# Rows of x for experts 1 to 7: spread over partition groups by DMA and transposed in 32x32 blocks on VectorE instead of on TensorE

## The chip, the cores and the metric

The kernel runs on one core of a Trainium2 chip. The core has five engines, each with its own instruction stream: TensorE (PE in the profile, its weight loads PEld), VectorE (DVE), ScalarE (ACT), GpSimd (POOL) and SyncE (SP), which here only issues DMAs. They meet through semaphores. The metric is the device time of one execution in microseconds; the time of a kernel is the median of its runs.

## The reference, cut to what matters

First a linear attention with decay (batch 4, 8 heads, 768 steps, head size 48) is computed; its output, 3072 rows of 384, is the x of a mixture of 8 experts. Every row goes to its two best experts:

```python
top2 = np.argpartition(-noisy_logits, 2, axis=1)[:, :2]
...
for e in range(E):
    for k in range(2):
        mask = top2[:, k] == e
        h = np.maximum(x[mask] @ w1[e], 0.0)          # 384 -> 1024
        out[mask] += top2_w[mask, k, None] * (h @ w2[e])   # 1024 -> 384
```

Everything is float32. The change is in the expert part.

## The kernel before, in words

**Attention part, up to about 190 us.** 24 blocks of 128 rows go through the attention; each block's x is stored to a DRAM table `xd`, with the routing weights (gates) beside it, 392 numbers a row. Router and sorting are worked in between. They end, for each expert, in lists of row numbers (`GR`, for gathers from `xd`) and token numbers (`TK`, for scatters to `out`).

**Expert part.** An expert takes up to 832 rows, as 6 tiles of 128 rows and one of 64. Tiles are put together in chunks: expert 0 has the chunks (0,1), (2,3), (4,5,6), named here (0,0), (0,1), (0,2); every other expert e has (e,0) with tiles 0 to 2, 384 rows wide, and (e,1) with tiles 3 to 6, 448 wide. For a chunk there are these steps:

- `xgather` (L733, POOL): one indirect DMA per tile fetches its rows from `xd` into an `xg` buffer, row by row on partitions. There are 6 such buffers, used in turn.
- `xT` (L760 to L763): three 128x128 transposes per tile on TensorE into PSUM (`ptm`). ACT rounds the result to fp32r (`xh`, L761), DVE subtracts for the rest (`xl`, L762), so that x = xh + xl in two parts that TensorE takes at its one-pass rate. ACT copies the tile's gates to `GT` (L763). `xT` is a generator of one tile at a time.
- `p1` (L781 to L785): for each of 8 groups f of 128 hidden columns, 9 matmuls (3 slices of the 384 features, times three products of high and low parts) go into one of three PSUM buffers `ph`. ACT takes the relu into `hb` (L783; the 64-wide tile's piece is `ht`), DVE makes the low part (L785).
- `p2` (L806 to L819): per tile 24 matmuls (16 for the 64-row tile) with W2 into `pym` (two buffers), evicted by ACT to `ot`.
- `emit_out` (L830 to L834): DVE multiplies by the gate and, from expert 1 on, adds `pv`, what `out` held so far for those tokens; POOL scatters the rows to `out`. `pgather` (L742, POOL) fetches the next expert's `pv` after the expert's last scatter.
- `w_split`, `wstep` (L273 to L279): an expert's weights come in 7 units, three of W1 (128 rows of 1024, 512 KB) and four of W2 (384 KB). A unit is a load by SP into one of three buffers `stg`, three calls of `wstep` later a rounding copy on ACT (`w0h` or `w1h`), one call later a subtraction on DVE. At most three units are under way.

**The order.** The kernel schedules by hand: each engine, SP and POOL included, works in the order in which the program names its instructions. The loop goes over chunks s = 2, 3, ... of the list (0,0), (0,1), (0,2), (1,0), (1,1), (2,0), ...: `p1` of chunk s with a `wstep` after each group; then `xgather` of chunk s+2; then `p2` of chunk s with a `wstep` after each tile. `xT` of chunk s+1 takes two tiles in `p1` (after groups j = 4 and 5, `XT_AT`), the rest one after each tile of `p2`. The next expert's W1 units are queued in an expert's first chunk, its W2 units in the second. Before the loop stands the hand-over from the attention part: three `wstep`s for expert 1's weights, `xgather(1, 0)`, then `p2(0, 1)` with `xT(0, 2)` after its last tile and two `wstep`s after each tile. So expert 1's first W2 unit, its fourth unit in all, is loaded by the first `wstep` after that `xT(0, 2)`, and copied by ACT after group 1 of `p1(0, 2)`.

Of the kernel before, what the change touches and what calls it, by code (L numbers as in the profile page):

```python
# [9 lines left out]
F32 = mybir.dt.float32  # L10
F32R = mybir.dt.float32r
# [3 lines left out]
AF = mybir.ActivationFunctionType  # L15
# [18 lines left out]
WARM3 = 1  # L34
NLD = 4
XT_AT_0 = 4
XT_AT = 4
LREP = 6
NOT = 4

# [2 lines left out]
def kernel(  # L43
# [14 lines left out]
    nc = tc.nc  # L58
    B, H, S, D = r.shape
    N, E = noise.shape  # L60
    DM = H * D
# [4 lines left out]
    ND = DM // 128  # L66
# [3 lines left out]
    NM = 6  # L70
# [3 lines left out]
    WMAX = 3 * 128 + TAIL  # L74
# [4 lines left out]
    NJ = NM + 1  # L79
    XW = DM + E  # L80
# [179 lines left out]
    def w_split(e):  # L260
        W[e] = {}
        units = []

        def unit(mat, c0, c1, src):
            def f():
                if mat not in W[e]:
                    sh = [128, ND, FF] if mat == 0 else [128, NF, DM]
                    W[e][mat] = [wpool[e % 2].tile(sh, F32R, name=f"w{mat}{x}{e % 2}", bufs=1) for x in "hl"]
                hi, lo = (t[:, c0:c1, :] for t in W[e][mat])
                t = stg.tile([128, 1024], F32, name="stg")  # L270
                n = hi.shape[1] * hi.shape[2]
                tv = t[:, :n].rearrange("p (a b) -> p a b", b=hi.shape[2])
                nc.sync.dma_start(tv, src)  # L273
                yield
                yield
                yield
                nc.scalar.activation(hi, tv, AF.Copy)
                yield
                nc.vector.tensor_sub(lo, tv, hi.bitcast(F32))  # L279
                yield  # L280
            return f()

        for c in range(ND):
            units.append(unit(0, c, c + 1, w1[e, c * 128:(c + 1) * 128, :].rearrange("(c p) f -> p c f", p=128)))
        for c in range(0, NF, 2):
            units.append(unit(1, c, c + 2, w2[e, c * 128:(c + 2) * 128, :].rearrange("(c p) d -> p c d", p=128)))
        return units
# [434 lines left out]
    def tw(t):  # L722
        return TAIL if t == NM else 128

    XG, XH, HH, PV, OT, scat_of = {}, {}, {}, {}, {}, {}
    def chunks(e):
        return CHUNKS1 if e else CHUNKS0

    def xgather(e, ci, early_=False):
        for t in chunks(e)[ci]:  # L730
            n = tw(t)
            xg = moe.tile([128, XW], F32, name="xg", bufs=6)
            nc.gpsimd.indirect_dma_start(  # L733
                out=xg[:n], out_offset=None, in_=xd[:GROUPS[GEARLY - 1][1] * 128] if early_ else xd,
                in_offset=bass.IndirectOffsetOnAxis(ap=GR[:n, e * NJ + t:e * NJ + t + 1], axis=0))
            XG[e, t] = xg

    def pgather(e):
        for t in range(NM + 1):
# [4 lines left out]
                in_offset=bass.IndirectOffsetOnAxis(ap=GA[:n, e * NJ + t:e * NJ + t + 1], axis=0))  # L744
            PV[e, t] = pv

    def xT(e, ci):
        xh = moe.tile([128, ND, WMAX], F32R, name="xh")
        xl = moe.tile([128, ND, WMAX], F32R, name="xl")
        XH[e, ci] = (xh, xl)  # L750
        o = 0
        for t in chunks(e)[ci]:
            n = tw(t)
            if (e, t) == (0, NM):
                pt = psum.tile([128, ND, 128], F32, name="ptm", tag=f"py{np2[0] % 2}")
                np2[0] += 1
            else:
                pt = psum.tile([128, ND, 128], F32, name="ptm", tag="pt", bufs=2)
            for d in range(ND):
                nc.tensor.transpose(pt[:, d, :n], XG[e, t][:n, d * 128:(d + 1) * 128], ident[:n, :n])  # L760
            nc.scalar.activation(xh[:, :, o:o + n], pt[:, :, :n], AF.Copy)  # L761
            nc.vector.tensor_sub(xl[:, :, o:o + n], pt[:, :, :n], xh[:, :, o:o + n].bitcast(F32))  # L762
            nc.scalar.activation(GT[:n, e * NJ + t:e * NJ + t + 1], XG[e, t][:n, DM + e:DM + e + 1], AF.Copy)  # L763
            o += n
            yield

    def p1(e, ci):
        w_ = sum(tw(t) for t in chunks(e)[ci])
        xh, xl = XH[e, ci]
        wh, wl = W[e][0]  # L770
        wb = w_ // 128 * 128
        hb = moe.tile([128, NF, 2, 3 * 128], F32R, name="hb", bufs=1)
        ht = moe.tile([128, NF, 2, TAIL], F32R, name="ht", bufs=1) if w_ > wb else None
        HH[e, ci] = (hb, ht)
        parts = [(hb[:, :, :, :wb], 0, wb)] + ([(ht, wb, w_)] if w_ > wb else [])
        for f in range(NF):
            fs = slice(f * 128, (f + 1) * 128)
            ph = psum.tile([128, WMAX], F32, name="ph", tag="pa", bufs=3)
            q = [(a, x, d) for d in range(ND) for a, x in ((wh, xh), (wh, xl), (wl, xh))]
            for j, (a, x, d) in enumerate(q):  # L780
                nc.tensor.matmul(ph[:, :w_], a[:, d, fs], x[:, d, :w_], start=(j == 0), stop=(j == len(q) - 1))  # L781
            for h_, a, b in parts:
                nc.scalar.activation(h_[:, f, 0, :], ph[:, a:b], AF.Relu)  # L783
            for h_, a, b in parts:
                nc.vector.scalar_tensor_tensor(h_[:, f, 1, :], ph[:, a:b], 0.0, h_[:, f, 0, :].bitcast(F32),  # L785
                                               op0=ALU.max, op1=ALU.subtract)
            yield

    np2 = [0]
# [73 lines left out]
    def rstep(n):  # L863

        for _ in range(n):
            while route_q:
                if at_pe[0] > 0:
                    at_pe[0] -= 1
                    if at_pe[0] > 0:
                        return  # L870
                try:
                    if next(route_q[0]) == "pe":
                        at_pe[0] = gap[0]
                        return
                    break
                except StopIteration:
                    route_q.pop(0)
            if not route_q:
                return
# [11 lines left out]
    for i in range(NT):  # L891
        if i + NLD - 1 < NT and i + NLD - 1 > 2:
            load(i + NLD - 1)
        if i >= NT - 16:
            q = (i - NT + 16) * 192
            nc.sync.dma_start(out[q:q + 192, :].rearrange("(p two) d -> p two d", two=2),
                              zrow[:96, None, :].to_broadcast([96, 2, DM]))
        if i + 1 < NT:
            trans(i + 1)
        if i:  # L900
            xtrans(i - 1)
            zup(i - 1)
        if i == I_EARLY:
            while GEARLY - 1 not in routed:
                rstep(1)
            early()
        if i + 1 < NT:
            uterm_b(i + 1)
        if i + 2 < NT:
            prep_k(i + 2)  # L910
            uterm_a(i + 2)
        wstep()
        rstep(STEPS_A)
        if i == 0:
            flag = consts_c()
        if i in (0, 3):
            next(flag)
        yout(i)
        xout(i)
        if i:  # L920
            logits(i - 1)
            route_when_done(i - 1)
        rstep(STEPS_B)
        if i == NT - 1:
            for _ in xT(0, 0):
                pass
            p1a = p1(0, 0)
        if i + 1 < NT:
            scores(i + 1)
            mask(i + 1)  # L930
        kvup(i)
        rstep(STEPS_KV)
# [7 lines left out]
    for j, _ in enumerate(p1a):  # L940
        if j == XT_AT_0:
            for _ in xT(0, 1):
                pass
        rstep(STEPS_P1)
    for t in p2(0, 0):
        rstep(STEPS_P2)
# [21 lines left out]
    wq.extend(w_split(1))  # L968
    for _ in range(3):
        wstep()  # L970
    xgather(1, 0)
    for t in p2(0, 1):
        if t == 3:
            for _ in xT(0, 2):
                pass
        hold.append((0, t))
        wstep()
        wstep()
    for s in range(2, len(seq)):
        e, ci = seq[s]  # L980
        end = s + 1 == len(seq)
        if e and ci == 0:
            nxt = w_split(e + 1) if e + 1 < E else []
            wq.extend(nxt[:ND])
        elif e:
            wq.extend(nxt[ND:])
        xt = xT(*seq[s + 1]) if not end else iter(())
        for j, _ in enumerate(p1(e, ci)):
            while hold:
                emit_out(*hold.pop(0))  # L990
            if XT_AT <= j < XT_AT + 2:
                next(xt, None)
            wstep()
        if s + 2 < len(seq):
            xgather(*seq[s + 2])

        for t in p2(e, ci):
            next(xt, None)
            wstep()
            hold.append((e, t))  # L1000
            while len(hold) > (0 if end else 1):
                emit_out(*hold.pop(0))
        if ci == len(chunks(e)) - 1 and not end:
            while hold:
                emit_out(*hold.pop(0))
            pgather(e + 1)
# [77 lines left out]
```

## Time and profile before

| | |
|---|---|
| median of 3 runs | 679.78 us (673.89, 679.78, 681.39) |
| profiled execution | 673.61 us, span 671.8 us from first to last instruction |
| mean granted TensorE clock | 0.968 |
| PE busy | 633.3 us, 94% of the span |
| DVE, ACT, POOL busy | 51%, 41%, 37% |
| transposes of x for the experts (L760) | 168 |
| DMA share, mean rate | 28.5% by SP's queue, 13.5% by POOL's; 117 GB/s |

A row of the profile's groups names line, engine, operation, output<-inputs and count, then busy time and mean duration. Matmuls are pipelined: the sum of their durations is more than the time that they take from PE, and the chain of waits shows the latter. "Released by" in brackets is what ended an engine's idle time. Durations are of one execution.

### The profile page before, as it was taken

The page shows a single profiled execution, that of the slowest core. Times are in us where ns is not written, and L with a number is a line of the kernel's source. Part 1 is how long each engine was busy: PE and PEld are TensorE (multiplying, and loading weights), DVE is VectorE, ACT ScalarE, POOL GpSimd, SP SyncE. Part 2 cuts the span into 40 slices and gives each one's busy share as a digit, 9 for nine tenths or more (in the row PEclk, how much of TensorE's full clock was granted, in tenths as well). Part 3 has the DMA queues.
Part 4 walks back from the last instruction along what each step waited for, and adds up shares of the span by engine and source line. Part 5 has one row for each costly group of instructions (what it writes and reads, how often), then busy time and mean ns, then how long its engine had stood idle before and what let it go on. Part 6 is the DMA issues. An engine that isn't in the chain of part 4 may idle for free.

```text
span 671.8 us, 11840 instructions
## 1 busy us (share of the span) xinstructions
PE 633.3 (94%) x4420; PEld 605.5 (90%) x4421; DVE 344.7 (51%) x837; ACT 278.2 (41%) x809; POOL 251.6 (37%) x318
## 2 busy tenths in 40 slices
PE   7998789897999799999999999999999999999993
PEld 4998788887889799999999999999999999999993
DVE  7675996678547673452525425344362534424230
ACT  4897556655332253252423414244242524422220
POOL 7465323524120353621741442264154236315111
PEclk9999888978699999999999999999999999999997
DMA  7999445734120572532524254262424426302001
GB/s 126 211 220 224 121 115 132 186 86 112 60 91 1 166 251 71 172 119 89 172 86 145 67 164 140 68 184 71 148 89 131 139 68 184 101 27 84 36 4 35
DMA packets 111445, 78.87 MB, mean 117 GB/s; under 512 B 86721, under 2 KB 101441, under 8 KB 111378
## 3 DMA queue, kind: packets, MB, share of 16 engines
q1 hardware_dynamic: 101442, 49.19, 28.5%
q0 software_dynamic: 9936, 28.83, 13.5%
q8 instruction: 37, 0.61, 0.4%
q14 instruction: 30, 0.25, 0.1%
HBM read 59.03 MB, written 19.76 MB: 117 GB/s over the span
## 4 chain that ended last, share of the span: by engine, by line
PE 68%; DVE 2%; ACT 0%; issue 0%; POOL 0%; POOLq 0%
PE ph L781 31%; PE pym L815 30%; PE ptm L760 3%; PE pym L808 2%; PE pym L806 2%; DVE r_oa L579 0%; DVE xl L762 0%; DVE hb L785 0%; PE py L388 0%; PE pl L418 0%; DVE r_ob L586 0%; DVE r_ob L582 0%; ACT xh L761 0%; POOL out_dram L834 0%; PE py L380 0%
## 5 line engine op out<-in xcount | busy, mean ns | idle before, releaser
L815 PE MATMUL pym<-w1h,hb 128*128 128x384 f32 x768 | 204.2, 339 | 0.0
L781 PE MATMUL ph<-xh,w0h 128*128 128x384 f32 (+3 forms) x408 | 141.6, 347 | 1.2 <-ACT xh L761 1.2
L815 PEld LDWEIGHTS pym<-w1h,hb 128*128 128x128 f32 x768 | 139.5, 188 | 0.6
L781 PE MATMUL ph<-xl,w0h 128*128 128x384 f32 (+3 forms) x408 | 138.8, 340 | 0.3 <-DVE xl L762 0.2
L781 PE MATMUL ph<-xh,w0l 128*128 128x384 f32 (+3 forms) x408 | 138.8, 340 | 0.0
L834 POOL DMA_INDIRECT out_dram<-ot,TK x56 | 57.1, 1020 | 216.1 <-DVE ot L830 198.1
L815 PE MATMUL pym<-w1l,hb 128*128 128x384 f32 x384 | 129.2, 336 | 0.0
L785 DVE SCALAR_TENSOR_TENSOR hb<-ph,hb 128x384 fp32r<-128x384 f32 (+1 forms) x136 | 72.3, 532 | 110.2 <-ACT ht L783 70.3
L783 ACT ACTIVATE hb<-ph 128x384 fp32r<-128x384 f32 (+1 forms) x136 | 64.2, 472 | 113.7 <-PE ph L781 111.7
L819 ACT ACTIVATE ot<-pym 128x384 f32<-128x384 f32 x45 | 22.1, 491 | 160.5 <-PE pym L815 160.5
L733 POOL DMA_INDIRECT xg<-xd,GR x56 | 55.1, 984 | 76.7 <-DVE ti L614 37.3
L781 PEld LDWEIGHTS ph<-xh,w0h 128*128 128x128 f32 x408 | 76.7, 188 | 4.1 <-ACT xh L761 1.5
L781 PEld LDWEIGHTS ph<-xl,w0h 128*128 128x128 f32 x408 | 76.7, 188 | 3.2 <-DVE xl L762 0.8
L781 PEld LDWEIGHTS ph<-xh,w0l 128*128 128x128 f32 x408 | 76.6, 188 | 2.6
L815 PEld LDWEIGHTS pym<-w1l,hb 128*128 128x128 f32 x384 | 72.2, 188 | 0.1
L762 DVE TENSOR_TENSOR xl<-ptm,xh 128x384 fp32r<-128x384 f32 (+1 forms) x56 | 29.0, 524 | 81.3 <-ACT xh L761 81.3
L388 PE MATMUL py<-vt,am 128*128 128x96 f32 x384 | 63.3, 296 | 5.6 <-DVE am L346 5.2
L742 POOL DMA_INDIRECT pv<-out_dram,GA x49 | 55.7, 1138 | 28.2 <-issue 13.7
L388 PEld LDWEIGHTS py<-vt,am 128*128 128x128 f32 x384 | 55.8, 211 | 6.5 <-DVE am L346 6.4
L304 POOL TENSOR_TENSOR kd<-kt,tabk 128x384 f32<-128x384 f32 x23 | 24.9, 1083 | 86.0 <-PE pwarm L356 72.5
L319 ACT ACTIVATE cv<-vt,c 128x48 f32<-128x48 f32 x192 | 45.9, 321 | 5.0 <-DVE c L316 4.7
L346 DVE TENSOR_TENSOR am<-pa,mneg 128x512 int32<-128x512 int32 x48 | 30.9, 684 | 15.8 <-PE pa L338 15.8
(196 smaller groups left out, 868.9 us busy)
## 6 DMA issues: line engine op xcount, KB each, us to landing
stg<-in_moe_w_dram SPq DMA_DIRECT2D x24, 512.0 KB, 4.2
stg<-in_moe_w_dram SPq DMA_DIRECT2D x32, 384.0 KB, 3.6
rd<-in_r_dram SPq DMA_DIRECT2D x24, 192.0 KB, 3.9
vt<-in_v_dram SPq DMA_DIRECT2D x24, 192.0 KB, 3.7
xd<-x SPq DMA_DIRECT2D x24, 192.0 KB, 2.3
out_dram<-zrow SPq DMA_DIRECT2D x16, 288.0 KB, 3.6
kt<-in_k_dram SPq DMA_DIRECT2D x23, 192.0 KB, 3.8
xg<-xd,GR POOLq DMA_INDIRECT x56, 3.2
```

The lines of the kernel that those rows point to most:

```text
L304: (eng or nc.gpsimd).tensor_mul(kd[i % 3][:, :, :D], kt[i], tabk[:, :, :D])
L319: nc.scalar.activation(cv[:, h, :], vt[i][:, h, :], AF.Copy, scale=c8[:, h, :])
L346: nc.vector.tensor_tensor(am[:, s].bitcast(I32), pa[s].bitcast(I32), mneg.to_broadcast([128, NP, 128]), op=ALU.bitwise_and)
L388: nc.tensor.matmul(o2, AM[i][:, s, p, :], vt[i][:, h, None, :].to_broadcast([128, 2, D]), start=not c and h == 0, stop=h == H - 1, skip_gr ...
L733: nc.gpsimd.indirect_dma_start(out=xg[:n], out_offset=None, in_=xd[:GROUPS[GEARLY - 1][1] * 128] if early_ else xd, in_offset=bass.Indirec ...
L742: nc.gpsimd.indirect_dma_start(out=pv[:n], out_offset=None, in_=out, in_offset=bass.IndirectOffsetOnAxis(ap=GA[:n, e * NJ + t:e * NJ + t + ...
L762: nc.vector.tensor_sub(xl[:, :, o:o + n], pt[:, :, :n], xh[:, :, o:o + n].bitcast(F32))
L781: nc.tensor.matmul(ph[:, :w_], a[:, d, fs], x[:, d, :w_], start=(j == 0), stop=(j == len(q) - 1))
L783: nc.scalar.activation(h_[:, f, 0, :], ph[:, a:b], AF.Relu)
L785: nc.vector.scalar_tensor_tensor(h_[:, f, 1, :], ph[:, a:b], 0.0, h_[:, f, 0, :].bitcast(F32), op0=ALU.max, op1=ALU.subtract)
L815: nc.tensor.matmul(py, hb[:, f, a, hs], x[:, f, :], start=(j == 0), stop=(j == len(q) - 1))
L834: st = nc.gpsimd.indirect_dma_start(out=out, out_offset=bass.IndirectOffsetOnAxis(ap=TK[:n, q:q + 1], axis=0), in_=ot[:n], in_offset=None, ...
```

## The change

For experts 1 to 7 the rows of a chunk are transposed in another way. All tiles of a chunk are gathered into one `xg` tile (one buffer instead of six). `spread` then issues 16 DMAs on SP, 32 partitions each: partitions 32q to 32q+31 of `xg` hold the rows, and their features a·96 to a·96+95 go to partitions 32a to 32a+31 of a new tile `xq`. There DVE transposes all 32x32 blocks in place, one instruction per tile. Afterwards partition 32a+j holds feature a·96 + c·32 + j for c = 0, 1, 2, and W1's rows are loaded in that order, as four DMAs of 32 rows per unit instead of one of 128. Expert 0 keeps TensorE's transposes, with `xh` and `xl` in the new layout, and its W1 loads are four DMAs too. In that layout the moving operand of a `p1` matmul is runs of 32 columns, 96 apart, instead of one run.

The gate copies leave `xT` for a function `gate`. The order becomes: `spread` and `gate` of chunk s+2 stand at the end of chunk s, after its `p2`; `xT` takes its two tiles of `p1` after groups 6 and 7, and none in `p1(0, 2)`; `xgather(1, 0)` and `spread(1, 0)` stand after `xT(0, 2)` and `gate(0, 2)` in `p2(0, 1)`, ahead of the two `wstep`s there; `gate(1, 0)` stands at the end of `p2(0, 2)`. `xgather(1, 1)` still stands after `p1(0, 2)`; as it takes the one `xg` buffer, it waits for all readers of the chunk before, `gate(1, 0)` among them.

```diff
-XT_AT = 4
+XT_AT = 6
...
-                nc.sync.dma_start(tv, src)
+                if mat:
+                    nc.sync.dma_start(tv, src)
+                else:
+                    for a in range(4):
+                        nc.sync.dma_start(tv[32 * a:32 * a + 32, 0, :], src[a])
...
-            units.append(unit(0, c, c + 1, w1[e, c * 128:(c + 1) * 128, :].rearrange("(c p) f -> p c f", p=128)))
+            units.append(unit(0, c, c + 1, w1[e].rearrange(f"{'(a c j)' if e else '(c a j)'} f -> c a j f", a=4, j=32)[c]))
...
     def xgather(e, ci, early_=False):
+        if (e, ci) != (0, 1):
+            xgt[0] = moe.tile([128, 4, XW], F32, name="xg", bufs=1)
         for t in chunks(e)[ci]:
             n = tw(t)
-            xg = moe.tile([128, XW], F32, name="xg", bufs=6)
+            xg = xgt[0][:, t if e == 0 and ci < 2 else t - chunks(e)[ci][0]]
...
+    def spread(e, ci):
+
+        xq = moe.tile([128, WMAX // 32, 96], F32, name="xq", bufs=1)
+        XQ[e, ci] = xq
+        w_ = sum(tw(t) for t in chunks(e)[ci]) // 32
+        for q in range(4):
+            m = (w_ - q + 3) // 4
+            for a in range(4):
+                nc.sync.dma_start(xq[32 * a:32 * a + 32, q:w_:4],
+                                  XGT[e, ci][32 * q:32 * q + 32, :m, a * 96:(a + 1) * 96])
+
+    def gate(e, ci):
+        for t in chunks(e)[ci]:
+            n = tw(t)
+            nc.scalar.activation(GT[:n, e * NJ + t:e * NJ + t + 1], XG[e, t][:n, DM + e:DM + e + 1], AF.Copy)
+
     def xT(e, ci):
-        xh = moe.tile([128, ND, WMAX], F32R, name="xh")
-        xl = moe.tile([128, ND, WMAX], F32R, name="xl")
+        xh = moe.tile([128, WMAX // 32, 96], F32R, name="xh")
+        xl = moe.tile([128, WMAX // 32, 96], F32R, name="xl")
...
+            if e:
+                v = XQ[e, ci][:, g].rearrange("p t (c j) -> p t c j", j=32)
+                nc.vector.transpose(v, v)
+                v, h, l = XQ[e, ci][:, g], xh[:, g], xl[:, g]
             else:
...
+            nc.scalar.activation(h, v, AF.Copy)
+            nc.vector.tensor_sub(l, v, h.bitcast(F32))
...
-                nc.tensor.matmul(ph[:, :w_], a[:, d, fs], x[:, d, :w_], start=(j == 0), stop=(j == len(q) - 1))
+                nc.tensor.matmul(ph[:, :w_], a[:, d, fs], x[:, :w_ // 32, d * 32:(d + 1) * 32], start=(j == 0), stop=(j == len(q) - 1))
...
-    xgather(1, 0)
     for t in p2(0, 1):
         if t == 3:
             for _ in xT(0, 2):
                 pass
+            gate(0, 2)
+            xgather(1, 0)
+            spread(1, 0)
         hold.append((0, t))
         wstep()
         wstep()
...
-            if XT_AT <= j < XT_AT + 2:
+            if XT_AT <= j < XT_AT + 2 and s > 2:
                 next(xt, None)
...
+            if s == 2 and t == NM:
+                gate(1, 0)
+        if s + 2 < len(seq):
+            spread(*seq[s + 2])
+            gate(*seq[s + 2])
```

More of the change, by code (lines that the diff above doesn't have):

```diff
@@ L727, in chunks @@
         return CHUNKS1 if e else CHUNKS0
+    xgt = [None]
+    XGT = {}
     def xgather(e, ci, early_=False):
+        if (e, ci) != (0, 1):
+            xgt[0] = moe.tile([128, 4, XW], F32, name="xg", bufs=1)
         for t in chunks(e)[ci]:
             n = tw(t)
-            xg = moe.tile([128, XW], F32, name="xg", bufs=6)
+            xg = xgt[0][:, t if e == 0 and ci < 2 else t - chunks(e)[ci][0]]
             nc.gpsimd.indirect_dma_start(
@@ L736, in xgather @@
             XG[e, t] = xg
+        XGT[e, ci] = xgt[0]
     def pgather(e):
@@ L745, in pgather @@
             PV[e, t] = pv
+    XQ = {}
+    def spread(e, ci):
[11 more added lines that the diff above has]
+            nc.scalar.activation(GT[:n, e * NJ + t:e * NJ + t + 1], XG[e, t][:n, DM + e:DM + e + 1], AF.Copy)
     def xT(e, ci):
-        xh = moe.tile([128, ND, WMAX], F32R, name="xh")
-        xl = moe.tile([128, ND, WMAX], F32R, name="xl")
+        xh = moe.tile([128, WMAX // 32, 96], F32R, name="xh")
+        xl = moe.tile([128, WMAX // 32, 96], F32R, name="xl")
         XH[e, ci] = (xh, xl)
@@ L753, in xT @@
             n = tw(t)
-            if (e, t) == (0, NM):
-                pt = psum.tile([128, ND, 128], F32, name="ptm", tag=f"py{np2[0] % 2}")
-                np2[0] += 1
-            else:
[L758 to L763, printed above, removed]
+            g = slice(o // 32, (o + n) // 32)
+            if e:
+                v = XQ[e, ci][:, g].rearrange("p t (c j) -> p t c j", j=32)
+                nc.vector.transpose(v, v)
+                v, h, l = XQ[e, ci][:, g], xh[:, g], xl[:, g]
+            else:
+                if (e, t) == (0, NM):
+                    pt = psum.tile([128, ND, 128], F32, name="ptm", tag=f"py{np2[0] % 2}")
+                    np2[0] += 1
+                else:
+                    pt = psum.tile([128, ND, 128], F32, name="ptm", tag="pt", bufs=2)
+                for d in range(ND):
+                    nc.tensor.transpose(pt[:, d, :n], XG[e, t][:n, d * 128:(d + 1) * 128], ident[:n, :n])
+                v = pt[:, :, :n].rearrange("p c (t i) -> p t c i", i=32)
+                h, l = (x[:, g].rearrange("p t (c i) -> p t c i", i=32) for x in (xh, xl))
+            nc.scalar.activation(h, v, AF.Copy)
+            nc.vector.tensor_sub(l, v, h.bitcast(F32))
             o += n
@@ L926 @@
                 pass
+            gate(0, 0)
             p1a = p1(0, 0)
@@ L943 @@
                 pass
+            gate(0, 1)
         rstep(STEPS_P1)
```

## The prediction

> **What bounds the kernel now.** I read the page first, for the span and the engines, then the busy time by stretches, then the chain of waits, and last the timelines of the queues between 222 and 290 us, where expert 0 hands over to expert 1.
>
> ```profile
> span 671.8 us, 11840 instructions
> PE 633.3 (94%) x4420; PEld 605.5 (90%) x4421; DVE 344.7 (51%) x837; ACT 278.2 (41%) x809; POOL 251.6 (37%) x318
> ...
> 257.00:285.00 28.00, 28.00 (x166) 27.38 (x165) 11.69 (x20) 9.93 (x22) 15.29 (x17) 1.00 0.41 125
> 285.00:316.00 31.00, 31.00 (x171) 29.45 (x170) 12.23 (x26) 11.15 (x30) 7.30 (x12) 1.00 0.36 113
> ```
>
> The two stretches (columns: length, then busy PE, PEld, DVE, ACT, POOL, then granted clock, DMA share, GB/s) are expert 1's two chunks. PE is busy all the time at full clock, DVE and ACT not half of it. So a PE instruction taken away there shortens the span, as long as nothing new keeps PE waiting. The chain of waits (start, length, what) gives the price of each PE step:
>
> ```profile
> 225.39 8.44 PE pym L815 x48
> ...
> 235.70 0.36 DVE xl L762
> 236.11 6.72 PE ph L781 x44
> ...
> 247.45 4.16 PE pym L815 x24
> ...
> 258.88 7.81 PE ph L781 x45
> ...
> 280.78 0.33 PE ptm L760 x3
> ...
> 285.47 9.15 PE ph L781 x45
> ```
>
> Three transposes of one row tile take 0.33 us from PE. A group f of p1 is 9 matmuls: 7.81/5 = 1.56 us in a 384-wide chunk, 9.15/5 = 1.83 us in a 448-wide one. A tile of p2 takes 4.16 us. Before 236.11 there is a hole: expert 0's last chunk waits for its transposed rows.
>
> **What is removed.** Experts 1 to 7 have 7 tiles each, so 49 × 0.33 = 16.2 us of PE work. The gate copies leave the chain before 236.11, worth perhaps 0.3 us: 16.5 us in all.
>
> **What is added off PE.** Each tile gets a transpose on DVE that the trace doesn't show. The nearest row with 384 columns is the subtraction L762 further down, 0.56 us, and I take 0.55, with half and twice that as bounds. DVE has 16 us free in the first stretch and 3 or 4 such to do, three `ph` buffers lie between it and PE, so they cost nothing. Without that cover a group would be late by the 0.55 us. xh and xl are then read from SBUF at unchanged sizes, which I take as no change. The moving operand of p1's matmuls (17 chunks × 8 × 9 = 1224) becomes runs of 32 elements. Nearest are matmuls of 96 columns, contiguous (L380) and in runs of 16 (L418):
>
> ```profile
> 190.69 0.22 PE py L380 x2
> 190.92 0.45 PE py L388 x4
> 191.36 0.67 PE pl L418 x6
> ```
>
> That is 0.11 us for each form, so I take 0. The rounding of these rows leaves 0.005 us either way, 1224 × 0.005 = 6 us; a gain I exclude, since no column less is streamed.
>
> **What is added to the queues, steady part.** SP carried only weight loads after the attention part. Now it carries 16 small DMAs per chunk (`spread`), and each W1 load as four. These are the rows for them (SP's timeline, the DMA list and one tile's durations min/median/max; KB each and us to landing):
>
> ```profile
> 12.86 2.25 SPq L136 DMA_DIRECT2D nz<-in_moe_noise_dram  x4
> L273 SPq DMA_DIRECT2D stg<-in_moe_w_dram x10: 328/368/379, 232.4 to 273.1; - x10
> stg<-in_moe_w_dram SPq DMA_DIRECT2D x7, 384.0 KB, 3.6
> stg<-in_moe_w_dram SPq DMA_DIRECT2D x3, 512.0 KB, 5.2
> xg<-xd,GR POOLq DMA_INDIRECT x13, 3.4
> 230.14 0.96 POOL L733 DMA_INDIRECT xg<-xd,GR  x1 [0.30 <-issue]
> 231.40 1.81 POOL L733 DMA_INDIRECT xg<-xd,GR  x1 [0.30 <-ACT w0h L277]
> 335.46 0.95 POOL L733 DMA_INDIRECT xg<-xd,GR  x1 [0.30 <-issue]
> 316.39 7.86 PE ph L781 x45
> ```
>
> An issue on SP takes 0.37 us; with a gap of 0.05 us 16 of them are 6.7 us (bounds: 0.33 each, 5.3 us; four of `nz` in 2.25 us, 0.56 each, 9.0 us). Gathers start 1.26 us apart. In a steady 384-wide chunk the last gather is issued at 335.46 − 316.39 = 19.1 us and lands at 22.5. The chunk then lasts 8 × 1.56 + 3 × 4.16 = 25.0 us, so spread ends at 29.2, 4.2 us into the next. The W2 load behind it lands 3.6 us on, at 7.8, and ACT wants it after group 3, at 4 × 1.83 = 7.3. Three `ph` buffers cover 5 us of that, so it costs nothing. In 448-wide chunks the gathers are earlier and spread ends before the chunk does. The gathered rows are wanted by DVE only at group 6. Four loads for one in expert 0's W1 lie on SP among prefetches three blocks ahead: nothing (1 us if that cover is gone).
>
> **Where PE will wait.** At the hand-over the cover is missing. SP, ACT and POOL take their work in program order.
>
> ```profile
> 237.58 0.38 ACT L783 ACTIVATE hb<-ph 128x256 fp32r<-128x256 f32 x1 [1.05 <-PE ph L781]
> 238.90 0.39 ACT L783 ACTIVATE hb<-ph 128x256 fp32r<-128x256 f32 x1 [0.82 <-PE ph L781]
> 239.28 0.85 ACT L277 ACTIVATE w1h<-stg 128x768 fp32r<-128x768 f32 x1
> 258.92 0.49 ACT L810 ACTIVATE ot<-pym 64x384 f32<-64x384 f32 x1 [2.29 <-PE pym L808]
> 252.55 0.56 DVE L762 TENSOR_TENSOR xl<-ptm,xh 128x384 fp32r<-128x384 f32 x1 [3.11 <-ACT xh L761]
> 261.01 0.56 DVE L785 SCALAR_TENSOR_TENSOR hb<-ph,hb 128x384 fp32r<-128x384 f32 x1 [0.36 <-ACT hb L783]
> 152.00:154.00 2.00, 0.38 (x10) 0.39 (x11) 2.00 (x9) 0.00 (x0) 1.33 (x2) 1.00 1.00 246
> 156.00:158.00 2.00, 2.00 (x11) 2.00 (x11) 1.93 (x12) 1.94 (x7) 0.00 (x0) 0.50 0.00 0
> 158.00:160.00 2.00, 2.00 (x19) 2.00 (x18) 0.45 (x2) 1.91 (x8) 0.00 (x0) 0.98 0.04 8
> ```
>
> A. With one `xg` buffer, expert 1's first gathers wait for gate(0,2), about 235.8; before, they were out at 230.14. The third starts at 238.3 and lands at 241.7. Spread(1,0) holds SP to 248.4. Behind it on SP stands the fourth unit of expert 1's weights, its first W2 load, landing 252.0. ACT copies that unit after group 1 of p1(0,2), at 239.28 in the row, and so stands still with every later eviction queued behind. PE fills three `ph` buffers at 1.32 us a group (237.58 to 238.90) and stops at 235.8 + 5 × 1.32 = 242.4. It goes on after the copy (0.85), a relu and a subtraction (0.38 and 0.56 in the rows, some 0.6 each with the 64-wide piece): 254.1. Idle 11.7 us (10.3 to 14.0 by SP's bounds). The last three rows show PE pausing at 152 to 154 us (0.38 us busy of 2) and a clock of 0.50 from 156 and 0.98 from 158 us. I take about 3 us at half speed after a long pause, another 1.5 us (0 to 2).
>
> B. xT(1,0) now runs in p2(0,2), its third tile after the last tile's eviction (0.49 on ACT, then an addition on DVE of L762's size). Then transpose 0.55, xh 0.49, xl 0.56: 2.6 us after p2's end, called E.
>
> C. xgather(1,1) waits for gate(1,0), E + 2.8. The four gathers start over 3.8 us and land at E + 10.0. gate(1,1) waits for them on ACT with all of p1(1,0)'s evictions behind. PE stops after three groups at E + 2.7 + 4.7 = E + 7.4 and resumes after relu and subtraction at E + 11.1: 3.7 us. POOL's scatters and expert 1's `pv` gathers queue behind too; their reader is p2(1,0), 20 us on.
>
> D. Spread(1,1) holds SP from E + 10.0 to 16.7, then expert 2's first W1 unit, four issues, to 18.4. I let it land at E + 21, between the landings above. ACT wants it after group 3, and copy (0.85 × 1024/768 = 1.1), relu (0.49) and subtraction (0.56) free the buffer at E + 23.1. PE is through group 6 at E + 11.1 + 4 × 1.56 = E + 17.4: 5.7 us, and about 2 us more for the clock or for the crowded DVE queue after it.
>
> Losses: 11.7 + 1.5 + 2.6 + 3.7 + 5.7 + 2 = 27.2 us, against 16.5 gained: 10.7 us slower. The profiled execution took 673.6 us, the median of the three runs is 679.8. The sum is 684.3 on the first and 690.5 on the second; I forecast 687.
>
> **Rivals.**
>
> 1, faster. ACT's copies are late by less than the buffers cover, because the issues go out much closer together or the loads land early; then only B stays: 673.6 − 16.5 + 2.6 = 659.7 us, 665.9 on the median. For it: PE is full in every steady chunk, so the 16.5 us are sure. Against it: even at 5.3 us of issuing A is 10.3 us. It decides below some 9 us of pauses. Chance 0.17.
>
> 2, faster, by the price of a transpose. Row: the 144 full ones take 23.0 us of busy time, 272 ns as a mean; 147 would be 40 us and the time 673.6 − 40 + 27.2 = 660.8.
>
> ```profile
> L760 PE MATMUL ptm<-ident,xg 128*128 128x128 f32 x144 | 23.0, 272 | 0.0
> ```
>
> The chain contradicts it, with three in 0.33 us. Chance 0.03. The Trainium skill, "TensorE: Matmul & The Clock Gate", Part 4, states about 275 ns for one in a kernel's context; the mean agrees with that length, the spacing in the chain doesn't make it a cost.
>
> 3, no change. The waits of C and D don't come, because gather (1,1) gets its buffer without waiting for gate(1,0). Then 16.5 stands against A and B, 15.8: 673 us, 679 on the median. Chance 0.20.
>
> 4, much slower. Either the strided operand costs its 6 us, 690 to 697 us, or each small DMA takes its landing, 2.5 us for one of `nz` (24 KB), one after another: 16 × 2.5 = 40 us where I have 6.7, 33 us more in A and in D each, over 750 us. The row of four issues in 2.25 us speaks against that. Chance 0.08. The Trainium skill, "DMA: Bandwidth & Descriptors", section "Rules for kernel authors", speaks against the change here: many small transfers should be coalesced, as under 64 KB one pays mostly overhead. By its fixed 2.0 us each an estimate for 16 in a row would be 32 us.
>
> ```profile
> nz<-in_moe_noise_dram SPq DMA_DIRECT2D x4, 24.0 KB, 2.5
> ```
>
> **How the numbers follow.** The forecast has 0.52, the rivals 0.17, 0.03, 0.20 and 0.08. About 1% (6.8 us) is what a measurement of this kernel can tell from no change. Slower: 0.52 + 0.08 = 0.60; within: 0.20; faster: 0.20. The forecast's own range is 680 to 697: pauses of 25 to 31 us on both bases. The range reaches down to rival 3 and the upper edge of rival 1, and up to the strided operand: 665 to 700 us.
>
> **What would show it.** L760 falls from 168 to 21 and expert 2's chunks last 25.0 and 29.9 us instead of 26.6 and 30.9: the gain. A: PE idle some 12 us within p1(0,2), ended by ACT L783, with ACT waiting for the DMA of `stg` in front of a w1h copy. C: ACT waiting for the gather at the gate copy before p1(1,0)'s first relu. D: ACT waiting for `stg` again after its fourth. I am wrong if PE has no pause over 5 us between 236 and 300 us, if p1's matmuls start further apart than 0.174 us at 384 columns, or if pauses come back with every expert.

## The result, and the profile after

The changed kernel takes 718.54 us (median of 4 runs, 715.16 to 724.01) against 680.59 us for the kernel before beside it: a ratio of 1.060, 95% interval 1.051 to 1.068. The forecast was 687 us, range 665 to 700: the result lies outside the range. The direction was right; the loss is 38 us where 10.7 were forecast.

The profiled execution took 717.44 us. Its page begins so:

```profile
span 715.6 us, 12025 instructions
...
PE 633.4 (89%) x4273; PEld 603.9 (84%) x4274; DVE 368.9 (52%) x886; ACT 280.6 (39%) x809; POOL 247.1 (35%) x318
```

The groups show that 147 of the 168 transposes are gone from PE (L795 is now their line):

```profile
L795 PE MATMUL ptm<-ident,xg 128*128 128x128 f32 (+1 forms) x21 | 2.8, 267 | 0.0
```

Yet PE is busy as long as before, 633.4 us in a span 43.8 us longer: it both stands still and works at a lower clock. The stretches of the hand-over show where. First the kernel before (p1(0,2), p2(0,2), p1(1,0), p2(1,0); columns as in the prediction: length, busy PE, PEld, DVE, ACT, POOL, clock, DMA share, GB/s):

```profile
235.56:247.29 11.73, 11.59 (x79) 11.35 (x79) 11.07 (x27) 8.21 (x24) 6.56 (x9) 1.00 0.70 211
247.29:258.72 11.43, 11.43 (x70) 11.10 (x68) 2.31 (x5) 2.06 (x7) 3.50 (x6) 1.00 0.53 191
258.72:271.89 13.17, 13.17 (x79) 13.10 (x79) 8.08 (x15) 7.69 (x15) 7.72 (x8) 1.00 0.31 88
271.89:285.30 13.41, 13.41 (x79) 13.05 (x79) 3.62 (x7) 2.24 (x7) 7.82 (x11) 1.00 0.55 175
```

The same four stages of the changed kernel:

```profile
238.50:266.76 28.26, 13.29 (x72) 12.84 (x73) 10.34 (x25) 7.30 (x22) 7.33 (x11) 0.70 0.42 126
266.76:280.38 13.62, 11.42 (x67) 10.77 (x65) 4.91 (x11) 3.48 (x11) 0.00 (x0) 1.00 0.01 1
280.38:309.38 29.00, 16.34 (x72) 15.46 (x73) 5.91 (x11) 5.65 (x15) 16.59 (x21) 0.77 0.70 178
309.38:326.40 17.02, 14.93 (x73) 14.29 (x73) 7.72 (x14) 4.51 (x9) 1.84 (x3) 0.89 0.07 20
```

They took 49.74 us and take 87.90: 38.2 us more. The rest of the expert part, from p1(1,1) to PE's last instruction, took 375.7 us and takes 378.4, although it has 42 transposed tiles fewer on PE. The remaining 2.9 us of the 43.8 lie ahead of p1(0,2), 2.4 of them in the attention part, whose end (the start of p1(0,0)) lies between 192.3 and 196.4 us in the nine profiles of this study.

The waits between 200 and 715 us (in all, times, longest) name what stands behind both: ACT waits for weight loads and gathers. For the kernel before, the same view lists no wait of ACT for a DMA after 225 us.

```profile
ACT w1h L281 <- DMA stg<-in_moe_w_dram: 41.2, 9, 16.1
ACT w0h L281 <- DMA stg<-in_moe_w_dram: 26.6, 16, 11.7
ACT GT L773 <- DMA xg<-xd,GR: 5.4, 3, 3.4
```

And this is ACT's timeline at the longest of them: A, C and D of the prediction, and one that it did not have, in chunk (2,1).

```profile
258.61 0.84 ACT L281 ACTIVATE w1h<-stg 128x768 fp32r<-128x768 f32 x1 [16.11 <-DMA stg<-in_moe_w_dram]
...
283.98 0.20 ACT L773 ACTIVATE GT<-xg 128x1 f32<-128x1 f32 x1 [3.37 <-DMA xg<-xd,GR]
...
304.26 1.06 ACT L281 ACTIVATE w0h<-stg 128x1024 fp32r<-128x1024 f32 x1 [11.65 <-DMA stg<-in_moe_w_dram]
...
398.11 0.84 ACT L281 ACTIVATE w1h<-stg 128x768 fp32r<-128x768 f32 x1 [6.34 <-DMA stg<-in_moe_w_dram]
```

SP's timeline shows what lay ahead of those loads:

```profile
244.62 10.65 SPq L767 DMA_DIRECT2D xq<-xg  x16
255.37 6.37 SPq L274 DMA_DIRECT2D stg<-in_moe_w_dram  x4
287.74 10.26 SPq L767 DMA_DIRECT2D xq<-xg  x16
298.05 6.51 SPq L277 DMA_DIRECT2D stg<-in_moe_w_dram  x12
...
383.84 10.71 SPq L767 DMA_DIRECT2D xq<-xg  x16
394.59 6.87 SPq L274 DMA_DIRECT2D stg<-in_moe_w_dram  x4
```

A spread holds SP for 10.3 to 10.7 us, not 6.7. The tile's own rows (min/median/max ns) give the price of one issue, and that of DVE's transpose:

```profile
L767 SPq DMA_DIRECT2D xq<-xg x224: 587/598/1232, 244.6 to 650.7; - x112
L786 DVE STREAM_TRANSPOSE xq<-xq x49: 370/569/579, 268.8 to 667.9; 128x384 f32<-128x384 f32 x42, 128x192 f32<-128x192 f32 x7
```

### The profile page after: what moved, and what is told of

It is laid out like the page before. It is cut to its first block, busy times and chain, and to the rows that moved or that the text cites. A ratio compares the mean times of both kernels' runs of the same rounds, so it can differ in the third digit from the quotient of the medians.

```text
span 715.6 us, 12025 instructions
## 1 busy us (share of the span) xinstructions
PE 633.4 (89%) x4273; PEld 603.9 (84%) x4274; DVE 368.9 (52%) x886; ACT 280.6 (39%) x809; POOL 247.1 (35%) x318
## 4 chain that ended last, share of the span: by engine, by line
PE 35%; SPq 20%; DVE 16%; issue 11%; DMA 10%; ACT 5%; POOL 1%; another core or an unknown queue 1%; DVEq 0%; POOLq 0%; ACTq 0%
SPq L767 17%; PE pym L851 11%; DMA stg<-in_moe_w_dram 8%; PE ph L817 6%; PE py L392 5%; PE pa L342 3%; PE pt L330 3%; SPq L277 2%; PE py L384 2%; ACT xh L798 2%; DVE hb L821 2%; PE pl L422 2%; DVE w1l L283 2%; DVE xq L786 2%; DVE xl L799 1%
## 5 line engine op out<-in xcount | busy, mean ns | idle before, releaser
L817 PE MATMUL ph<-xl,w0h 128*128 128x384 f32 (+3 forms) x408 | 142.0, 348 | 0.7 <-DVE xl L799 0.7
L817 PE MATMUL ph<-xh,w0l 128*128 128x384 f32 (+3 forms) x408 | 141.8, 348 | 0.0
L817 PEld LDWEIGHTS ph<-xh,w0h 128*128 128x128 f32 x408 | 79.1, 194 | 45.3 <-issue 34.1
L817 PEld LDWEIGHTS ph<-xl,w0h 128*128 128x128 f32 x408 | 79.1, 194 | 3.9 <-DVE xl L799 1.4
L817 PEld LDWEIGHTS ph<-xh,w0l 128*128 128x128 f32 x408 | 79.2, 194 | 2.5
L752 POOL DMA_INDIRECT pv<-out_dram,GA x49 | 53.1, 1085 | 39.1 <-issue 19.4
L799 DVE TENSOR_TENSOR xl<-xq,xh 128x384 fp32r<-128x384 f32 (+1 forms) x49 | 25.9, 530 | 51.0 <-ACT xh L798 46.8
L798 ACT ACTIVATE xh<-xq 128x384 fp32r<-128x384 f32 (+1 forms) x49 | 24.5, 501 | 54.2 <-DVE xq L786 52.2
```

Of the source, the lines that this page charges most:

```text
L752: nc.gpsimd.indirect_dma_start(out=pv[:n], out_offset=None, in_=out, in_offset=bass.IndirectOffsetOnAxis(ap=GA[:n, e * NJ + t:e * NJ + t + ...
L798: nc.scalar.activation(h, v, AF.Copy)
L799: nc.vector.tensor_sub(l, v, h.bitcast(F32))
L817: nc.tensor.matmul(ph[:, :w_], a[:, d, fs], x[:, :w_ // 32, d * 32:(d + 1) * 32], start=(j == 0), stop=(j == len(q) - 1))
```

## The experiments

The theory after the result: the loss is made of weight loads that stand behind a spread on SP, so that ACT reaches their copies first, with PE's evictions queued behind; at the hand-over it is larger because the gathers are late too. The rivals: the W1 loads in quarters, the single `xg` buffer, the strided operand, or something that only follows from the hand-over.

**W1 loads in quarters, alone.** The kernel before, with each W1 load as four DMAs and nothing else.

```diff
-                nc.sync.dma_start(tv, src)
+                if mat:
+                    nc.sync.dma_start(tv, src)
+                else:
+                    for a in range(4):
+                        nc.sync.dma_start(tv[32 * a:32 * a + 32, 0, :], src[32 * a:32 * a + 32, 0, :])
```

> The kernel before, with each W1 load split into four DMAs of 32 rows and nothing else changed. Theory (the weight loads stand behind the small DMAs of spread on SP, and ACT stands behind the weight loads): three more issues of about 0.45 us per W1 unit meet an otherwise empty queue, so 680.6 to 683 us, no pause above 1 us. Rival (the quartered W1 loads themselves land too late for ACT's copies): 690 us or more, with ACT waiting for the DMA of stg in front of w0h copies in every expert.

Measured: 679.54 us, ratio 1.001 (0.998 to 1.004). The quarters cost nothing by themselves.

**The same bytes in one or two DMAs.** The changed kernel, with `spread`'s 16 DMAs replaced by one of 128 partitions (two in a 448-wide chunk).

```diff
-        for q in range(4):
-            m = (w_ - q + 3) // 4
-            for a in range(4):
-                nc.sync.dma_start(xq[32 * a:32 * a + 32, q:w_:4],
-                                  XGT[e, ci][32 * q:32 * q + 32, :m, a * 96:(a + 1) * 96])
+        nc.sync.dma_start(xq[:, :12].rearrange("p (t a) x -> p t (a x)", a=4), XGT[e, ci][:, :3, :DM])
+        if w_ > 12:
+            nc.sync.dma_start(xq[:, 12:14].rearrange("p t x -> p (t x)"), XGT[e, ci][:, 2, :192])
```

> The changed kernel, but spread moves the same number of bytes in one DMA of 128 partitions (a second small one for the 64-row tile) instead of 16 of 32 partitions; the rows are not rearranged, so x is wrong for experts 1 to 7, the work of the engines is the same. Theory (issue time on SP, 16 x 0.645 us): SP is free 9.5 us earlier in each chunk; p1(0,2) still waits for the gather of (1,0), some 7 us instead of 16.5, the second wait in p1(1,0) goes, the pauses of the later experts go: 685 to 692 us. Rival (the added traffic, 9 MB in packets of 384 bytes, slows the loads): 710 us or more. Rival (DVE's transposes hold up the evictions): 710 us or more too, since they are all still there.

Measured: 680.83 us, ratio 1.003 (1.000 to 1.006), less than the 685 to 692 us expected. The ratio falls from 1.060 to 1.003: nearly all of the loss hangs on the 16 small DMAs ahead of the loads, not on the number of bytes, nor on the operand's layout, DVE's transposes or the buffers, which are all still there. This run also moves longer pieces than the 384 bytes of `spread`; that the small pieces are not what slows the loads is shown by the next run, which keeps them. What is left of A in this run, a wait of 7.68 us instead of 16.11, comes from the late gathers: SP's timeline shows the spread at 242.42, until when it waited for them (the changed kernel's first one stood at 244.62), and the load right behind it.

```profile
242.42 0.69 SPq L764 DMA_DIRECT2D xq<-xg  x1
243.21 7.96 SPq L274 DMA_DIRECT2D stg<-in_moe_w_dram  x4
277.03 0.64 SPq L764 DMA_DIRECT2D xq<-xg  x1
277.71 0.64 SPq L766 DMA_DIRECT2D xq<-xg  x1
```

p1(0,2) takes 20.88 us here and p1(1,0) 18.02, against 28.26 and 29.00. Most of the 384- and 448-wide chunks after expert 1 take 25.2 to 25.3 and 30.1 us, so about the gain that was forecast per chunk is there, and it pays for most of what is left at the hand-over.

**Loads first.** The changed kernel with only SP's order changed: the next chunk's first three weight loads are issued ahead of the spread, and spread(1,0) goes after group 3 of p1(0,2).

```diff
-            spread(1, 0)
...
+            if s == 2 and j == 3:
+                spread(1, 0)
...
+            for un in wq[:3]:
+                loads[id(un)]()
         if s + 2 < len(seq):
             spread(*seq[s + 2])
```

> The changed kernel with another order on SP alone: the next chunk's first three weight loads are issued before spread, and spread(1,0) comes after group 3 of p1(0,2), behind expert 1's loads. All DMAs, sizes and counts are as in the changed kernel. Theory (order on SP): the pause in p1(0,2) goes (-16), the second one in p1(1,0) goes (-10), those of the later experts go (-14); the wait of ACT for the gather of (1,1) and the late third tile of xT(1,0) stay (some 7): 674 to 684 us. Rival (issue count or traffic, whatever the order; or DVE): 705 us or more.

Measured: 676.70 us, ratio 0.995 (0.992 to 0.998), as expected. The order alone takes the ratio from 1.060 to below 1, some 42 us. From p1(1,1) to the end it takes 363.5 us, 12.2 less than before (375.7), with the 384-wide chunks at 25.2 to 25.3 us (one at 26.2) and the 448-wide ones at 30.1 to 30.3. At the hand-over p1(0,2) takes 14.50, p2(0,2) 13.67, p1(1,0) 18.01 and p2(1,0) 15.55: 61.7 us against 49.7, which eats the gain.

**Loads first, and a second buffer for the rows.** The run before, with an `xg` buffer of its own for chunks (e,0), the gathers (1,0) at their old place, gate(1,0) ahead of p2(0,2), and xT(1,0) two tiles at a time in p2(0,2).

```diff
-            xgt[0] = moe.tile([128, 4, XW], F32, name="xg", bufs=1)
+            odd = e and ci == 0
+            xgt[0] = (late[0] if odd else moe).tile([128, 4, XW], F32, name="xo" if odd else "xg", bufs=1)
...
+    xgather(1, 0)
     for t in p2(0, 1):
...
+            if s == 2:
+                next(xt, None)
```

> As the run with the loads first, and with two buffers for the gathered rows, so that the gathers of (1,0) and (1,1) are issued as early as in the kernel before, gate(1,0) stands before p2(0,2), and xT(1,0) takes two tiles per tile of p2(0,2). Theory: all waits of the hand-over go and the 16.2 us of transposes are gained: 664 to 670 us, faster than both kernels. Rival (added traffic or DVE work costs something in every chunk): 675 us or more, with chunks of later experts longer than 25.3 and 30.2 us.

Measured: 676.49 us, ratio 0.996 (0.992 to 0.999), no better than without the buffer; the expectation missed. p1(1,0) fell to 13.01 us, but p2(1,0) rose to 19.17. Spread(1,0) had moved no earlier (SP issued it from 248.93 to 260.6, behind a weight load that waits for its `stg` buffer), and twice in 35 us ACT's timeline shows it standing for over 4 us in the middle of relus, with no wait of its own in the trace ("remote": no instruction of this core is found as the releaser):

```profile
256.51 0.39 ACT L833 ACTIVATE hb<-ph 128x256 fp32r<-128x256 f32 x1 [4.66 <-remote]
...
287.51 0.49 ACT L833 ACTIVATE hb<-ph 128x384 fp32r<-128x384 f32 x1 [4.33 <-remote]
```

The waits of ACT that carry this mark come to 29.8 us in this run from 200 us on. The spread is not what they need: the kernel before with W1 in quarters has one of 3.72 us at its hand-over, the run with loads first one of 3.90 us at 287.67, and the three runs below have none. The two shown, 9.0 us together, are about what the four stages of the hand-over take more here (58.9 us) than in the run with TensorE for expert 1 (50.2). So this run does not show that the second buffer is worth nothing at the hand-over with loads first. What the stops are stays open (last section).

**The second buffer alone.** The changed kernel in its own SP order, with the second `xg` buffer, the gathers (1,0) at their old place and gate(1,0) ahead of the gathers (1,1).

```diff
+            xgt[0] = (late[0] if odd else moe).tile([128, 4, XW], F32, name="xo" if odd else "xg", bufs=1)
...
+    xgather(1, 0)
     for t in p2(0, 1):
...
-            xgather(1, 0)
...
+        if s == 2:
+            gate(1, 0)
         if s + 2 < len(seq):
             xgather(*seq[s + 2])
...
-            if s == 2 and t == NM:
-                gate(1, 0)
```

> The changed kernel with one thing taken away: the single xg buffer at the hand-over. Chunk (1,0) gets a buffer of its own, its gathers go out at their old place (before p2(0,1)), and gate(1,0) stands ahead of the gathers (1,1). The order on SP stays, with each spread ahead of the weight loads. Theory (each pause is a weight copy that ACT reaches before a load behind a spread has landed, and the spread is late by what its gathers wait for): spread(1,0) goes out some 8 us earlier, so the wait of ACT's w1h copy in p1(0,2) falls from 16.1 to about 8 us; the wait at gate(1,1), 3.4 us, is gone; spread(1,1) can start with xT(1,0) done, some 7 us earlier, so the wait of the w0h copy in p1(1,0) falls from 11.7 to about 5; the recurring pauses in the later chunks stay. 700 us (695 to 705). Rival (the single buffer matters little, the 32-partition DMAs alone make the loads late): within 5 us of the changed kernel, 714 to 720.

Measured: 719.34 us, ratio 1.070 (1.063 to 1.076) against 673.66 for the kernel before beside it: no gain, and the 700 us missed. The stages tell why. The hand-over did get shorter, 76.1 us instead of 87.9: the wait in A is 11.79 us instead of 16.11 and the one in D 8.64 instead of 11.65, and that at gate(1,1) is gone. But from p1(1,1) to the end it takes 395.0 us, 16.6 more than the changed kernel. With two buffers POOL fetches the rows of the next chunk while the late weight load is on its way. SP's and ACT's timeline in chunk (2,1), then the stretch between issue and copy:

```profile
368.02 11.15 SPq L768 DMA_DIRECT2D xq<-xo  x16
379.22 9.13 SPq L274 DMA_DIRECT2D stg<-in_moe_w_dram  x4
```

```profile
385.00 0.84 ACT L281 ACTIVATE w1h<-stg 128x768 fp32r<-128x768 f32 x1 [7.65 <-DMA stg<-in_moe_w_dram]
```

```profile
379.20:385.00 5.80, 2.99 (x15) 2.42 (x13) 0.00 (x0) 0.01 (x1) 0.33 (x2) 1.00 0.86 247
```

From the last spread issue to the copy it is 5.8 us here, with the DMA engines 86% busy. In the changed kernel it was 3.5 us (394.59 to 398.11):

```profile
394.60:398.10 3.50, 2.01 (x10) 1.50 (x9) 0.00 (x0) 0.00 (x0) 0.99 (x1) 1.00 0.68 203
```

The same stretch is longer in all six 448-wide chunks up to (6,1): 4.1 to 6.0 us here, 3.3 to 3.6 in the changed kernel. That is about 11 of the 16.6 us. The gathers are the difference that the timelines show there; no run takes them alone out of that stretch. The single buffer, which I had taken for a cost only, also kept the gathers out of the loads' way.

**TensorE for expert 1.** The version that the runs before point to. Expert 1 keeps TensorE's transposes, the old order of steps and expert 0's order of W1's rows; experts 2 to 7 go the new way, loads first, with two `xg` buffers. The diff is against the run with loads first and two buffers, cut to its core.

```diff
-            if e:
+            if e > 1:
                 v = XQ[e, ci][:, g].rearrange("p t (c j) -> p t c j", j=32)
...
-            if XT_AT <= j < XT_AT + 2 and s > 2:
+            at = 4 if s < 4 else XT_AT
+            if at <= j < at + 2:
...
-        if s + 2 < len(seq):
+        if 4 < s + 2 < len(seq):
             spread(*seq[s + 2])
             gate(*seq[s + 2])
```

> Expert 1 keeps TensorE's transposes and the old order too (gathers (1,0) early into a second xg buffer, no spread, no gate at the end of a chunk); experts 2 to 7 are transposed in the new way, with a chunk's first three weight loads issued ahead of its spread. Theory (the steady gain is real, and the hand-over is the only place that lacks the time for gather, spread and transpose): the chunks up to (1,1) take what they took before (p1(0,2) 11.7, p2(0,2) 11.4, p1(1,0) 13.2, p2(1,0) 13.4 us), from (2,0) on 25.3 and 30.1 us a chunk: 680.6 - 11.4 = 669 us (666 to 672), ratio 0.983. Rival (the hand-over is slow for what stands outside the new transposes: W1 loads in quarters, loads ahead of the spread, pauses of ACT without a releaser): no better than the run with loads first, 675 to 679.

Measured: 661.42 us against 673.66 beside it, ratio 0.982 (0.975 to 0.988). The ratio is the one expected (0.983); the time lies below the 666 to 672 us, as the kernel before was faster beside this run too. This is the fastest kernel of the study: it beats the kernel before and the changed one. Its spreads are still 16 DMAs each, so their number costs nothing that shows where the order leaves room. Whether expert 1 needs TensorE is not shown: the run with loads first and two buffers, which spreads expert 1 too, had the stops without a releaser at its hand-over, and this one had none. A variant with TensorE for chunk (1,0) alone gave no time. PE has no pause in it; the stretches are p1 and p2 of (1,1), then the chunks (2,0) and (2,1):

```profile
285.00:315.00 30.00, 30.00 (x161) 28.57 (x160) 13.79 (x29) 11.49 (x30) 7.05 (x10) 1.00 0.51 143
...
315.08:340.39 25.31, 25.31 (x145) 25.31 (x145) 14.04 (x24) 10.35 (x22) 14.61 (x17) 1.00 0.51 151
340.39:370.49 30.10, 30.10 (x161) 28.66 (x161) 13.79 (x29) 11.50 (x30) 7.49 (x12) 1.00 0.51 148
```

SP's timeline shows the order that does it: the spread has its 10 to 11 us behind the loads that ACT wants next, and in front of a stretch in which SP has nothing to do.

```profile
298.34 10.14 SPq L283 DMA_DIRECT2D stg<-in_moe_w_dram  x12
308.66 11.00 SPq L781 DMA_DIRECT2D xq<-xg  x16
325.45 5.21 SPq L280 DMA_DIRECT2D stg<-in_moe_w_dram  x3
337.53 10.69 SPq L781 DMA_DIRECT2D xq<-xo  x16
```

**The same, spread first.** The last run with SP's order of the changed kernel, to see the recurring part without the hand-over: only the `for un in wq[:3]` loop ahead of `spread` is taken out again.

> As the run with expert 1 on TensorE, but with SP's order of the changed kernel: each spread of experts 2 to 7 ahead of the next weight loads. It leaves the hand-over undisturbed and keeps only what recurs with every expert. Theory (the weight loads stand behind 16 issues of 0.645 us on SP, and ACT waits for the first of them in the middle of p1): the hand-over takes what it took before (p1(0,2) 11.9, p1(1,0) 13.2 us), and from (2,0) on pauses of 2 to 7 us stand in the 448-wide p1 and about 1 us in the 384-wide p2, so some 14 to 28 us more than with loads first: 661.4 x 1.03 = 682 us (675 to 690), ratio 1.00 to 1.025, with ACT waiting for stg at w1h copies. Rival (the recurring pauses are an after-effect of the late hand-over, which never catches up): no pauses from (2,0) on and 659 to 664 us, ratio 0.98.

Measured: 688.76 us, ratio 1.021 (1.015 to 1.028). The hand-over is undisturbed (p1(0,2) 11.85, p1(1,0) 13.17 us), but from p1(2,0) to the end it takes 361.8 us where loads first took 332.5: 29.3 us from SP's order alone. So the pauses recur by themselves and are no after-effect of the hand-over. (They come to more than the changed kernel's; like the run with the second buffer alone, this one has two `xg` buffers.) The waits from 330 us on, and the longest one on ACT's timeline:

```profile
ACT w1h L281 <- DMA stg<-in_moe_w_dram: 30.6, 8, 7.9
```

```profile
478.43 0.84 ACT L281 ACTIVATE w1h<-stg 128x768 fp32r<-128x768 f32 x1 [7.89 <-DMA stg<-in_moe_w_dram]
```

## Why the prediction was right and wrong

**The gain: right.** 42 tiles from (1,1) on at 0.33 us are 13.9 us. With expert 1 on TensorE, experts 2 to 7 take 332.5 us where they took 344.8, and (1,1), which no longer carries the transposes for (2,0), 30.2 where it took 30.9: 13.0 us. Rival 2 (272 ns a transpose) would have made that 34.3 us. The changed kernel itself shows no such chunks: expert 2's took 26.8 and 34.0 us, not 25.0 and 29.9, because the pauses below stand in them.

**Off PE: right.** DVE's transpose takes 0.569 us (0.55 assumed). The operand in runs of 32 costs nothing: p1 at 384 columns takes 12.5 to 12.6 us in the undisturbed chunks, 8 × 1.56 or 1.58. Both prices were also in the run with few DMAs.

**The step that failed: an issue of `spread` on SP.** The prediction took 0.37 us from the weight loads plus a gap, 16 in 6.7 us, with 5.3 to 9.0 as bounds. It is 0.60 us and 0.645 with the gap, 10.3 to 10.7 us, outside the bounds. The nearest row in the prediction was `nz`, 0.56 us, which it used as an upper bound only. These 3.6 to 4 us come up at each place where a load stands behind a spread:

- A: idle time of PE in p1(0,2) is 28.26 − 13.29 = 15.0 us, forecast 11.7. The clock's part, 13.29 − 11.59 = 1.7 us, was forecast as 1.5. The order of events was as described.
- B: 13.62 − 11.42 = 2.2 us, forecast 2.6. Right.
- C and D: PE stands for 29.00 − 16.34 = 12.7 us in p1(1,0), forecast 3.7 + 5.7 = 9.4. By slices of 1 us, C has 3.2 of it and D 9.3, so the excess is D's, the one of the two that has a spread ahead of it. The waits are the named ones (3.37 us at the gate copy for the gather; 11.65 us at the copy of expert 2's first W1 unit). The clock took 16.34 − 12.6 = 3.7 us instead of 2, and p2(1,0), at 17.02 us instead of 12.7, carried another 4 us of slow clock and short waits that were not in the sum.

For these four stages together the forecast was 27.2 us of losses less seven tiles' transposes and the gate copies, 24.6 us; 38.2 were measured, 13.6 more.

**The step that failed worse: the steady part "costs nothing".** The forecast had the spread end 4.2 us into the 448-wide chunk, the W2 load land at 7.8, ACT ask at 7.3, and three `ph` buffers cover the rest. In chunk (2,1), which begins at 383.66, the spread ends at 394.55, 10.9 us in; the load lands at 398.11, 14.4 in; ACT had asked at 391.77, 8.1 in. The landing, 3.5 us, was right (3.6). Of the 6.7 us by which the spread is late, 4.0 are SP's price; 2.7 are its start, which the prediction put 2.5 us before the end of the chunk, and which came 0.2 us after it, as POOL issued the third gather 23.7 us into the chunk (at 380.56 in one that began at 356.87), not 19.1: it stood behind expert 2's `pv` gathers, which began 9.9 us into the chunk instead of 6.4. 0.5 us of lateness against 5 us of cover had looked safe; 6.3 us is more than the cover, and PE stops.

Nor does the spread end before the chunk does in the 448-wide ones, as the prediction had it: the one in chunk (1,1) ends at 358.93, 2.1 us into chunk (2,0), and ACT waits for W1 loads there too. Over the experts the forecast gain of 13.9 us became a loss of 2.7, 16.6 us in all. Against the run with loads first 14.9 of them are pauses, 10.2 in the 448-wide chunks and 4.7 in the 384-wide ones; the rest is that this run gains 12.2 us and not 13.9. The run with the spread first shows that the pauses come without any late hand-over.

**The account of the profiled execution:** 10.7 forecast, 13.6 more at the hand-over, 16.6 recurring, and 2.9 ahead of p1(0,2) make 43.8 us, the difference of the spans. (The medians differ by 38 us; the profiled execution of the kernel before was faster than any of the four runs of its median.)

**The rivals.** 1 and 3 fell: the waits of A, C and D all came. The result lies between the forecast's 697 us and the over 750 of rival 4, where the prediction had no case: it let the price of an issue change only A, and the steady part not at all. The strided operand of rival 4 costs nothing, and its small DMAs are not issued one landing after another. The rule beside it, to coalesce many small transfers (the Trainium skill, "DMA: Bandwidth & Descriptors", section "Rules for kernel authors"), had the sign of the result. The run with the same bytes in one or two DMAs agrees with it. By that page's 2.0 us of fixed cost each, which it gives for DMAs issued by GpSimd, an estimate is 32 us for a spread; the traces have 10.3 to 10.7, so it was the issue on SP that cost here, and the measurement decides. The prediction had named "pauses that come back with every expert" as a sign that it is wrong; they did.

## What to carry to other kernels

Moving work from a full engine to an idle one pays only if what feeds it has room: here the gain was real (13 us measured), and small DMAs ahead of prefetches in an in-order queue cost over three times as much (42 us by the run with loads first). Put DMAs with slack behind those that some engine is about to wait for, and leave the old way where there is no slack yet (here at the hand-over to the first expert). The two together, with a second buffer for the rows, turned 1.060 into 0.982; the first alone gave 0.995, and what the second is worth is not settled. For an operation that the trace doesn't show and that repeats 16 times a chunk, take the dearest of the near rows into the forecast, not into its bound: `nz`'s 0.56 us was nearer to 0.60 than the loads' 0.37.

## What the runs showed of the hardware that was not expected

- A DMA from `xg` to `xq` held SP for about 0.60 us at both sizes tried: 0.598 us for 32 partitions (median of L767 above), and 0.606 us for 128 partitions with three tiles' rows in the run with few DMAs. So the size does not set this time here. What does is open: the weight loads from DRAM stood at 0.37 us before, but `nz`, from DRAM too, at 0.54, and the changed kernel's W1 loads of 32 partitions have a median of 0.42.

```profile
L764 SPq DMA_DIRECT2D xq<-xg x14: 605/606/687, 242.4 to 602.3; - x14
```

- After the long pause of A the clock stayed at half for longer than the 3 us taken, and the short pause of C was enough for it too. In the changed kernel PE stops at about 246 and works again from about 260.6, and the granted clock is 0.50 for over 4 us of that work, until about 265:

```profile
250.00:252.00 2.00, 0.00 (x0) 0.00 (x0) 0.00 (x0) 0.00 (x0) 0.00 (x0) 0.50 0.24 55
...
262.00:264.00 2.00, 2.00 (x9) 2.00 (x9) 2.00 (x5) 0.65 (x4) 0.00 (x0) 0.50 0.69 188
264.00:266.00 2.00, 2.00 (x11) 2.00 (x10) 0.44 (x2) 0.36 (x2) 0.00 (x0) 0.67 0.02 8
```

  In C PE stands for 3.2 us, from 285.8 to 289.0, and the clock falls after work has begun again:

```profile
286.00:288.00 2.00, 0.00 (x0) 0.00 (x0) 0.00 (x0) 0.54 (x3) 1.77 (x3) 1.00 0.48 145
...
290.00:292.00 2.00, 2.00 (x8) 2.00 (x7) 0.00 (x0) 0.00 (x0) 0.25 (x1) 0.50 0.43 95
```

- ACT's stops without a releaser, 4.66 and 4.33 us in the run with loads first and two buffers, one of 4.21 us in the changed kernel at 614 us, are not explained. Instruction fetch would be one candidate: the Trainium skill, "Runtime: NRT & Kernel Launch", section "Instruction fetch mechanics", says that engines fetch their instructions in blocks by DMA and that this is mostly hidden. No run here shows that it was this, and none was made to tell. The amount fetched does not tell the runs apart: the pages of the profile count the same 36 and 33 packets in the two instruction queues for the run with ten such stops from 200 us on and for the last three, which have none.
